# A sliding-window attention and gated MLP kernel: PSUM given out bank by bank, softmax sums of four heads together, V products in 32-column quarters, and every step's place written out

## Chip, core and metric

The kernel runs on one core of one Trainium2 chip. The metric is the device time of one execution in microseconds (us); lower is better. The kernel before takes 231.15 us, the median of three runs (230.51 to 231.65).

## What is computed

The reference, cut to what matters:

```python
# q, k, v: [8, 8, 576, 64] = batch, heads, positions, head width
scores = q @ k^T / 8                      # per batch and head
mask   = (0 <= i - j < 64)                # each position sees itself and the 63 before it
attn   = softmax(where(mask, scores, -1e9))
x      = attn @ v  -> [8, 576, 512]       # the eight heads side by side

h      = relu(x @ w_in)                   # w_in 512 x 1024
u, v2  = h[..., :512], h[..., 512:]
v_n    = (v2 - mean) / sqrt(var + 1e-6)   # per row of 512
v_s    = w_spatial @ v_n + b_spatial      # w_spatial 576 x 576, over the positions
out    = (u * v_s) @ w_out                # w_out 512 x 512, float32 [8, 576, 512]
```

Inputs and outputs are float32 in DRAM; the kernel computes in float16 with float32 sums in PSUM.

## The kernel before, in words

**Steps.** The work is cut into named steps, about 1,100 for the eight batches `b`. A step is one instruction, or for TensorE a run of matmuls. The names are used below, so here they are in the order in which a batch goes through them. A batch's eight heads come in two halves `g` of four heads; of a batch's 576 positions, 512 go in the main steps and the last 64 in steps with `r` in place of `g` ("remainder").

| step | engine | what it does | line |
|---|---|---|---|
| `ldk`, `ldq`, `ldv` | DMA on SP's queue | loads of one half's k and q (576 KB each) and v (five pieces) | L296, L320 |
| `ck`, `cq`, `cv` | POOL (also DVE, ACT in the first two batches) | float32 to float16 | L219, L217 |
| `sl`, `su`, `s4` | the same | a copy `hs` of v, shifted by 64 positions | L219 |
| `tk`, `tq` | DVE | transposes of k and q | L306 |
| `S` | PE | scores of four heads: 64 matmuls of 32x64 tiles into two PSUM tiles `sc` of two banks | L366, L430 |
| `E` | ACT | exp of a pair of heads, 128x1024, two per half | L374, L440 |
| `M` | DVE | minimum with the mask, in place, two per half | L377, L444 |
| `P` | PE | for a pair of heads: sums by a matrix of ones (`oz<-e,onesK`, two matmuls of 512 columns) and the products with v (16 matmuls of 128x64 weights, 64 columns) | L389, L394 |
| `N`, `n` | ACT | logarithm of the sums, exp of minus that: 1/sum, 128x512, one of each per pair | L409, L411 |
| `X` | DVE | product times 1/sum, gives `x` | L413 |
| `V`, `Vr`, `Vb`, `Va` | PE, ACT, DVE, DVE | second half of `x @ w_in`; relu; row statistics (two) | L506, L486, L488, L490 |
| `L1`, `L2`, `A` | ACT, ACT, DVE | 1/standard deviation, then normalised rows `vn`, five `A` | L531, L533, L543 |
| `U`, `Ur` | PE, ACT | first half of `x @ w_in`; relu | L559, L572 |
| `G`, `Ge` | PE, DVE | `w_spatial @ v_n + b`; times `u` | L589, L603 |
| `O`, `Oe`, `st` | PE, ACT, DMA | `@ w_out`; copy out of PSUM; store | L614, L477, L479 |

`V`, `U`, `G` and `O` have index 0 to 3 for full blocks of 128 and 4 for the 64-wide rest. All `A` of a batch come before its first `G`, since `G` sums over all positions. `V` and `U` need all `X` of the batch.

**Weights.** `ldwin`/`cwin` load and convert w_in (eight pieces of 256 KB), `ldwsp`/`cwsp` w_spatial, `W`/`We` transpose it on PE, `ldwo`/`cwo` load w_out. They share a staging ring `wst` of two buffers.

**Buffers.** PSUM has eight banks of 512 float32 per partition. Here four of them are two tiles `ring` of two banks each, used by turns for the scores (`sc`) and for sums and products (`oz`: bank 0 products, bank 1 sums), and four are single tiles `mm`, taken in turn by V, U, G, O and the transposes. So the four-head score step `S` takes the whole ring, and the next user waits until `E` or `X` has read it.

**What sets the order.** Each engine executes its instructions in program order and waits on semaphores. The program order is chosen by a planner (`Plan.order`, L63 to L115): a list scheduler that gives each step an estimated cost, and at each turn takes the step that could start first by these estimates and by the number of free buffers (`BUFS`, L21); ties go by a due time (`key`). Where a step may run on several engines (conversions of the first two batches) it also chooses the engine. A ring tile is given to the `S` or `P` step that the planner takes next.

Of the kernel before, what the change touches and what calls it, by code (L numbers as in the profile page):

```python
# [14 lines left out]
S = 576  # L15
BIG = 65504.0

BUFS = {"nat": 5, "natv": 3, "hqk": 3, "qkT": 6, "hv": 4, "hs": 4, "e2": 3, "ring": 2, "mm": 4,  # L21
        "lnz": 2, "zinv": 2, "x": 2, "x4": 2, "vs": 10, "st6": 6, "vn": 10, "ru": 6, "g": 10,
        "ob": 4, "wst": 2, "ln": 2}
AFTER = {"PE": 0.16, "ACT": 0.1, "DVE": 0.1, "POOL": 0.12, "DQ": 2.0}
MODE_CHANGE = 0.095


class Buf:
    __slots__ = ("tag", "users", "t", "make", "ready")

    def __init__(self, tag, make):
        self.tag, self.make, self.users, self.t = tag, make, [], None


class Op:
    __slots__ = ("engs", "key", "fn", "deps", "acq", "mode", "eng", "start", "end", "left", "outs",
                 "n", "name")

    def __init__(self, name, engs, key, fn, deps, acq, uses, mode):
        self.name, self.engs, self.key, self.fn, self.mode = name, engs, key, fn, mode  # L40
        self.acq, self.eng, self.start, self.end = acq, None, None, None
        self.deps = [d for d in deps if d is not None]
        self.outs = []
        self.left = len(self.deps)
        for d in self.deps:
            d.outs.append(self)
        for b in list(uses) + list(acq):
            b.users.append(self)


class Plan:
    def __init__(self):
        self.ops = []

    def add(self, name, engs, key, fn, deps=(), acq=(), uses=(), mode=None):
        if isinstance(engs, tuple):
            engs = [engs]
        op = Op(name, engs, key, fn, list(deps), list(acq), list(uses), mode)
        op.n = len(self.ops)
        self.ops.append(op)  # L60
        return op

    def order(self, free):  # L63
        free = dict(free)
        taken = {t: [] for t in BUFS}
        avail = [o for o in self.ops if o.left == 0]
        mode = None
        done = []
        while avail:
            best = None  # L70
            for o in avail:
                t0 = 0.0
                for d in o.deps:
                    t = d.end + AFTER[d.eng]
                    if t > t0:
                        t0 = t
                want = {}
                for b in o.acq:
                    i = len(taken[b.tag]) + want.get(b.tag, 0)
                    want[b.tag] = want.get(b.tag, 0) + 1  # L80
                    if i >= BUFS[b.tag]:
                        for u in taken[b.tag][i - BUFS[b.tag]].users:
                            if u.end is None:
                                t0 = None
                                break
                            t0 = max(t0, u.end + 0.1)
                    if t0 is None:
                        break
                if t0 is None:
                    continue  # L90
                e, c = min(o.engs, key=lambda ec: max(free[ec[0]], t0) + ec[1])
                t = max(free[e], t0)
                rank = (t, o.key, o.n)
                if best is None or rank < best[0]:
                    best = (rank, o, e, c, t)
            assert best is not None, "no step can go"

            _, o, e, c, t = best
            if e == "PE" and o.mode is not None:
                if mode is not None and o.mode != mode:  # L100
                    c += MODE_CHANGE
                mode = o.mode
            o.eng, o.start, o.end = e, t, t + c
            free[e] = t + c
            for b in o.acq:
                taken[b.tag].append(b)
            avail.remove(o)
            done.append(o)
            for x in o.outs:
                x.left -= 1  # L110
                if x.left == 0:
                    avail.append(x)
        assert len(done) == len(self.ops), "steps left over"
        done.sort(key=lambda o: (o.start, o.n if o.eng is None else 0))
        return done  # L115
# [3 lines left out]
def kernel(  # L119
# [27 lines left out]


    scratch = cpool.tile([128, 512], f16, name="scratch")
    nc.vector.memset(scratch[:], 0.0)  # L150
    warm = psp.tile([128, 512], f32, tag="mm", bufs=BUFS["mm"], name="warm")
    for _ in range(16):
        nc.tensor.matmul(warm[:, :], scratch[:, 0:128], scratch[:, :], start=True, stop=True)

    onesK = cpool.tile([128, 64], f16, name="onesK")
    nc.vector.memset(onesK[:], 1.0)
# [11 lines left out]
    maskr = cpool.tile([128, 8, 64], f16, name="maskr")  # L168
    for h in (0, 1):
        for u in range(8):  # L170
            if u % 2 == 1:
                nc.vector.tensor_copy(mask[:, h, u, :], keep[:])
            else:
                nc.vector.tensor_scalar(mask[:, h, u, :], keep[:], -1.0, BIG, ALU.mult, ALU.add)
        nc.vector.memset(mask[64:128, h, 0, :], 0.0)
    for u in range(8):
        nc.vector.tensor_copy(maskr[:, u, :], mask[:, 0, 2, :])
# [3 lines left out]
    for i in range(NSB):  # L181
        nc.vector.memset(mv_t[i][:], 1.0)
        nc.vector.memset(vn4_t[i][64:65, :], 1.0)
# [8 lines left out]
        "e2": ([128, 2, 512], f16), "lnz": ([128, 512], f32), "zinv": ([128, 512], f32),  # L192
        "x4": ([128, 256], f16), "vs": ([128, 512], f16), "st6": ([128, 8], f32),
        "vn": ([128, 512], f16), "ru": ([128, 512], f32), "g": ([128, 512], f16),
        "ob": ([128, 512], f32), "wst": ([128, 1024], f32), "ln": ([128, 10], f32),
    }

    def buf(tag, name):
        if tag == "ring":
            return Buf(tag, lambda: psp.tile([128, 2, 512], f32, tag="ring", bufs=2, name=name))  # L200
        if tag == "mm":
            return Buf(tag, lambda: psp.tile([128, 512], f32, tag="mm", bufs=BUFS["mm"], name=name))
        if tag[0] == "x" and tag != "x4":
            return Buf(tag, lambda: pool.tile([128, 512], f16, tag=tag, bufs=BUFS[tag], name=name))
        shape, d = SHAPES[tag]
        return Buf(tag, lambda: pool.tile(shape, d, tag=tag, bufs=BUFS[tag], name=name))

    for r in range(4):
        BUFS[f"x{r}x"] = 2
# [10 lines left out]


    WIN, WSP, WOUT = [], [], []

    def win_steps(key):
        for half in (1, 0):
            for r in range(4):
                st = buf("wst", f"wi{half}{r}")
                cs = slice(512 * half, 512 * half + 512)
                ld = add(f"ldwin{half}{r}", ("DQ", 0.68), key + 0.001 * (4 * (1 - half) + r),
                         lambda e, st=st, r=r, cs=cs: nc.sync.dma_start(  # L230
                             st.t[:, 0:512], moe_w_in[128 * r:128 * r + 128, cs]), acq=[st])
                WIN.append(add(f"cwin{half}{r}", [("ACT", 0.5), ("DVE", 0.43), ("POOL", 0.6)],
                               -1 + key + 0.001 * (4 * (1 - half) + r),
                               lambda e, st=st, r=r, cs=cs: cp(e, w_in_sb[r][:, cs], st.t[:, 0:512]),
                               deps=[ld], uses=[st]))

    def win_dep(half, r):
        return WIN[4 * (1 - half) + r]

    def wsp_steps(key):  # L240
        nat = []
        for t in range(5):
            tn = 128 if t < 4 else 64
            st = buf("wst", f"ws{t}")
            ld = add(f"ldwsp{t}", ("DQ", 0.75 if t < 4 else 0.4), key + 0.001 * t,
                     lambda e, st=st, t=t, tn=tn: nc.sync.dma_start(
                         st.t[0:tn, 0:576], moe_w_spatial[128 * t:128 * t + tn, :]), acq=[st])
            nat.append(add(f"cwsp{t}", [("ACT", 0.55), ("DVE", 0.47), ("POOL", 0.67)],
                           key + 0.001 * t,
                           lambda e, st=st, t=t, tn=tn: cp(e, wsp_nat[t][0:tn, :],  # L250
                                                           st.t[0:tn, 0:576]),
                           deps=[ld], uses=[st]))
        st = buf("wst", "wsb")
        ld = add("ldb", ("DQ", 0.1), key + 0.006, lambda e, st=st: nc.sync.dma_start(
            st.t[64:65, 0:576], moe_b_spatial[:].unsqueeze(0)), acq=[st])
# [389 lines left out]
    for o in order:  # L645
        for bf in o.acq:
            t = bf.make()
            if t is not None:
                bf.t = t
# [35 lines left out]
```

## Time and profile before

| what | value |
|---|---|
| runs before | 231.15, 231.65, 230.51 us |
| span of the profiled execution, first to last instruction | 228.4 us |
| median of the runs minus that span | 2.75 us |
| mean granted TensorE clock | 0.933 of full |
| busy POOL; 128x1024 exps `E` (32) on ACT | 84.1 us; 31.1 us |
| `N` of 128x512 (32) and `n` of 128x512 (32) on ACT | 19.3 and 20.4 us |
| bytes moved by DMA, mean rate | 42.67 MB, 187 GB/s |

The profile is of one execution; its own time as a run is not given apart from the span, so the 2.75 us stands for what lies around the span. "Busy" counts an instruction from start to end; matmuls overlap, so a run of matmuls is better read from one start to the next start than from the sum of durations. A "granted clock" of 0.50 in a stretch means that TensorE got half of its clock there.

Starts of `G0` of each batch in the chain that ended last and in the timeline of PE: 54.47, 78.8, 102.9, 126.3, 150.1, 173.5, 196.0 and 215.2 us. The last matmul ends near 224.7 us, and one copy and one store follow.

### The profile page before, as it was taken

How to read it: one execution, taken by the hardware profiler on the slowest of the kernel's cores; microseconds unless marked ns; L12 is line 12 of the kernel's file. 1: busy time of each engine (PE TensorE's matmuls, PEld its weight loads, DVE VectorE, ACT ScalarE, POOL GpSimd, SP SyncE). 2: the span in 40 equal slices, each digit the busy share in tenths (PEclk: the TensorE clock that was granted, in tenths of full speed). 3: DMA queues.
4: the chain of work that ended last, by engine and by line, in shares of the span. 5: the costliest groups of instructions: out<-in, count | busy, mean ns of one | idle time of the engine just before them, and what ended most of it. 6: DMA issues, size and time to landing. Idle time of an engine off the chain costs nothing.

```text
span 228.4 us, 6947 instructions
## 1 busy us (share of the span) xinstructions
PE 193.3 (85%) x2873; PEld 98.1 (43%) x2873; DVE 178.6 (78%) x341; ACT 157.1 (69%) x281; POOL 84.1 (37%) x124
## 2 busy tenths in 40 slices
PE   7413329886989997999899997999799999999993
PEld 2202224452544553454445453455345544554441
DVE  7896769998697788978989879988888686855640
ACT  3554564995469956797579676975696779758623
POOL 2001213252869645882488038913870000000000
PEclk9955556998899999999999999999999999999999
DMA  6999889799988999979689728511310041014005
GB/s 227 343 309 264 241 238 321 213 282 274 305 252 249 332 292 312 292 182 268 166 296 262 163 96 276 143 25 46 140 26 4 31 156 26 3 46 153 12 13 193
DMA packets 50417, 42.67 MB, mean 187 GB/s; under 512 B 39569, under 2 KB 39569, under 8 KB 50386
## 3 DMA queue, kind: packets, MB, share of 16 engines
q1 hardware_dynamic: 50386, 42.23, 62.8%
q8 instruction: 22, 0.36, 0.7%
q14 instruction: 9, 0.07, 0.1%
HBM read 32.79 MB, written 9.44 MB: 185 GB/s over the span
## 4 chain that ended last, share of the span: by engine, by line
PE 54%; DVE 17%; DMA 13%; ACT 8%; issue 4%; SPq 1%; POOL 0%; DVEq 0%; ACTq 0%; POOLq 0%
PE pg L589 16%; PE pv L506 8%; PE po L614 7%; PE pu L559 6%; DMA nq<-in_q_dram 6%; DVE qT L306 4%; PE sc L366 4%; DMA ws<-in_moe_w_spatial_dram 4%; DVE kT L306 3%; PE oz L389 3%; PE oz L394 2%; ACT e L374 2%; DMA wi<-in_moe_w_in_dram 2%; PE pg L595 2%; DMA wo<-in_moe_w_out_dram 2%
## 5 line engine op out<-in xcount | busy, mean ns | idle before, releaser
L219 POOL COPY hs<-hv 64x512 f16<-64x512 f16 x51 | 33.8, 665 | 25.1 <-ACT hv L217 10.6
L589 PE MATMUL pg<-wspT,vn 128*128 128x512 f16 (+1 forms) x160 | 39.4, 389 | 1.0 <-DVE vn L543 1.0
L374 ACT ACTIVATE e<-sc 128x1024 f16<-128x1024 f32 x32 | 31.1, 1022 | 4.3 <-PE sc L366 3.6
L506 PE MATMUL pv<-win,x 128*128 128x512 f16 x128 | 32.6, 395 | 0.0
L603 DVE TENSOR_TENSOR g<-pg,ru 128x512 f16<-128x512 f32 (+1 forms) x40 | 24.7, 634 | 9.1 <-PE pg L589 9.1
L377 DVE TENSOR_TENSOR e<-e,mask 128x1024 f16<-128x1024 f16 x32 | 26.8, 854 | 5.7 <-ACT e L374 5.7
L559 PE MATMUL pu<-x,win 128*128 128x512 f16 x128 | 31.0, 380 | 0.0
L477 ACT COPY ob<-po 128x512 f32<-128x512 f32 (+1 forms) x33 | 19.3, 585 | 16.4 <-PE po L614 15.4
L614 PE MATMUL po<-wout,g 128*128 128x512 f16 x128 | 30.5, 380 | 0.0
L409 ACT ACTIVATE ln<-oz 128x512 f32<-128x512 f32 x32 | 19.3, 602 | 16.1 <-PE oz L394 16.1
L488 DVE BATCH_NORM_STATS2 st<-vs 128x6 f32<-128x512 f16 (+1 forms) x40 | 26.9, 677 | 4.1 <-ACT vs L486 3.8
L486 ACT ACTIVATE vs<-pv 128x512 f16<-128x512 f32 (+1 forms) x40 | 23.5, 594 | 6.7 <-PE pv L506 5.5
L413 DVE TENSOR_TENSOR x<-oz,zi 128x512 f16<-128x512 f32 x32 | 21.8, 684 | 6.0 <-ACT zi L411 6.0
L219 POOL CAST hv<-nv 128x512 f16<-128x512 f32 x26 | 16.2, 644 | 26.7 <-DMA nv<-in_v_dram 13.8
L411 ACT ACTIVATE zi<-ln 128x512 f32<-128x512 f32 (+1 forms) x40 | 23.7, 593 | 0.9
L306 DVE STREAM_TRANSPOSE kT<-hk 128x576 f32<-128x576 f32 x16 | 20.0, 1250 | 3.6 <-PE scr L430 3.2
L366 PE MATMUL sc<-qT,kT 32*64 32x128 f16 (+2 forms) x1024 | 13.8, 231 | 9.1 <-DVE x L413 8.0
L589 PEld LDWEIGHTS <-vn 128*128 128x128 f16 (+1 forms) x160 | 13.9, 98 | 17.7 <-DVE vn L543 4.8
L572 ACT ACTIVATE ru<-pu 128x512 f32<-128x512 f32 (+1 forms) x40 | 20.6, 571 | 0.8 <-PE pu L559 0.8
L306 DVE STREAM_TRANSPOSE qT<-hq 128x576 f32<-128x576 f32 x16 | 19.9, 1244 | 0.3 <-ACT hq L217 0.3
L219 POOL CAST hk<-nk 128x1152 f16<-128x1152 f32 x12 | 13.7, 1143 | 16.7 <-DMA nk<-in_k_dram 8.5
L389 PE MATMUL oz<-e,onesK 128*64 128x512 f16 x64 | 14.1, 435 | 6.1 <-DVE e L377 6.1
(79 smaller groups left out, 274.3 us busy)
## 6 DMA issues: line engine op xcount, KB each, us to landing
nk<-in_k_dram SPq DMA_DIRECT2D x16, 576.0 KB, 5.4
nq<-in_q_dram SPq DMA_DIRECT2D x16, 576.0 KB, 6.0
nv<-in_v_dram SPq DMA_DIRECT2D x64, 128.0 KB, 5.2
out_dram<-ob SPq DMA_DIRECT2D x32, 256.0 KB, 2.2
wi<-in_moe_w_in_dram SPq DMA_DIRECT2D x8, 256.0 KB, 4.5
ws<-in_moe_w_spatial_dram SPq DMA_DIRECT2D x4, 288.0 KB, 4.2
nv<-in_v_dram SPq DMA_DIRECT2D x16, 64.0 KB, 4.2
wo<-in_moe_w_out_dram SPq DMA_DIRECT2D x4, 256.0 KB, 3.8
```

The lines of the kernel that those rows point to most:

```text
L219: ENG[e].tensor_copy(o, i)
L306: d = add(f"t{name}{b}_{g}", ("DVE", 0.68), key, lambda e: nc.vector.transpose(qt.t[:, :].rearrange("p (i j) -> p j i", j=18), h.t[:, :].b ...
L374: ex = add(f"E{b}_{g}{u}", ("ACT", 0.91), key, lambda e, u=u: nc.scalar.activation(e2[u].t[:, :, :], sc[u].t[:, :, :], AF.Exp, bias=0.0, s ...
L377: mins.append(add(f"M{b}_{g}{u}", ("DVE", 0.58), key, lambda e, u=u: nc.vector.tensor_tensor(e2[u].t[:, :, :], e2[u].t[:, :, :], mask[:, : ...
L411: c = add(f"n{b}_{r}", ("ACT", 0.09 + 0.0008 * n), key, lambda e: nc.scalar.activation(zi.t[:, 0:n], lz.t[:, 0:n], AF.Exp, bias=0.0, scale ...
L486: rl = add(f"Vr{b}_{j}", ("ACT", 0.5), key, lambda e: nc.scalar.activation(vs.t[0:jn, :], m.t[0:jn, :], AF.Relu), deps=[pv], acq=[vs], use ...
L488: s1 = add(f"Vb{b}_{j}", ("DVE", 0.7), key + 0.02, lambda e: nc.vector.bn_stats(st6.t[0:jn, 0:6], vs.t[0:jn, :]), deps=[rl], acq=[st6], us ...
L506: nc.tensor.matmul(m.t[:, :], XB[b, r].t[:, 128 * j:128 * j + 128], w_in_sb[r][:, 512:1024], start=(r == 0), stop=(r == 3))
L559: nc.tensor.matmul(m.t[:, :], w_in_sb[r][:, 128 * i:128 * i + 128], XB[b, r].t[:, :], start=(r == 0), stop=(r == 3))
L589: nc.tensor.matmul(m.t[:, :], w[0:kn, 128 * i:128 * i + 128], wspT[kk][0:kn, 0:512], start=(kk == 0), stop=(kk == 4))
L603: lambda e, m=m, g=g, ru=ru, n=n: nc.vector.tensor_tensor(g.t[:, 0:n], m.t[:, 0:n], ru.t[:, 0:n], ALU.mult),
L614: nc.tensor.matmul(m.t[:, :], G[r][0].t[:, 128 * j:128 * j + 128], w_out_sb[r][:, :], start=(r == 0), stop=(r == 3))
```

## The change

1. **PSUM** is four tiles of two banks made once (`PAIR`), and each PE step is told its banks: the number after the colon in the written order, e.g. `S0_0:PE:0:1` (two pairs: banks 0 to 3) or `P0_0:PE:6:5`. In the written order `S` always has pairs 0 and 1, and everything else shares banks 4 to 7.
2. **Sums.** A new step `Z` makes the sums of four heads in one bank: four matmuls, each with a 128x32 matrix of ones and 512 columns, into partitions 0, 32, 64 and 96 upward. `N` and `n` then run once per half, not once per pair, and both `X` of the half use the one result.
3. **V products.** `P` covers four heads: each head's v is split into even and odd columns (`vhalf`), 32 wide, so `P` is 64 matmuls of 128x32 weights and 64 columns into two banks, in place of two times 16 of 128x64. A half's `x` is one tile [128, 2, 512]; w_in's rows are loaded in the order that this gives (`(p two) c -> p two c`).
4. **Order.** `Plan.order` goes. `ORDER` is a list of all 1,029 steps, with engine and banks, that is emitted as it stands.
5. Smaller: w_in and w_out come in loads of 512 KB (six in place of twelve) and `wst` has three buffers; v of batches 2 to 7 is converted and shifted in one piece per half (4 POOL instructions in place of 7); `vs` and `vn` have 8 buffers (were 10), `e2` 4 (were 3), the remainder's `er` has 2 of its own; the mask is made in 9 instructions (were 26).

The diff, cut to its core:

```diff
+ORDER = """
+ldk0_0:DQ
+ldq0_0:DQ
+...
+S0_0:PE:0:1
+...
+"""
+def as_listed(plan):
+    by = {s.name: s for s in plan.steps}
+    out = []
+    for word in ORDER.split():
+        name, eng, *banks = word.split(":")
+        out.append((by.pop(name), eng, [int(x) for x in banks]))
+    return out
...
+    PAIR = [psp.tile([128, 2, 512], f32, name=f"ps{i}") for i in range(4)]
+    def bank(j):
+        return PAIR[j // 2][:, j % 2, :]
...
+    def vhalf(t, c, hh, f):
+        return t[:, c, hh, :].rearrange("p (d two) -> p two d", two=2)[:, f, :]
...
-        s = add(f"S{b}_{g}", ("PE", 0.5), key, emit_S, deps=[DKT[b, g], DQT[b, g], LASTP[0]],
-                acq=sc, uses=[KT[b, g], QT[b, g]], mode="s")
+        s = add(f"S{b}_{g}", ("PE", 0.53), key, emit_S, deps=[DKT[b, g], DQT[b, g]],
+                acq=sc + e2, uses=[KT[b, g], QT[b, g]], mode="s")
...
-                    for h in (0, 1):
-                        nc.tensor.matmul(oz.t[64 * h:64 * h + 64, 1, :], onesK[:, :], ee[:, h, :],
-                                         start=True, stop=True)
-                    for c in range(8):
-                        for h in (0, 1):
-                            vv = vn if c % 2 == 1 or c == 0 else vs
-                            nc.tensor.matmul(oz.t[64 * h:64 * h + 64, 0, 64 * c:64 * c + 64],
-                                             vv[:, c // 2, 2 * u + h, :],
-                                             ee[:, h, 64 * c:64 * c + 64], start=True, stop=True)
+        def emit_Z(e):
+                for hh in range(4):
+                    nc.tensor.matmul(zb.t[32 * hh:32 * hh + 32, :], ones[:, :],
+                                     e2[hh // 2].t[:, hh % 2, :], start=True, stop=True)
+        def emit_P(e):
+                for f in (0, 1):
+                    for c in range(8):
+                        vv = hv if c % 2 == 1 or c == 0 else hs
+                        for hh in range(4):
+                            nc.tensor.matmul(ob[f].t[32 * hh:32 * hh + 32, 64 * c:64 * c + 64],
+                                             vhalf(vv, c // 2, hh, f),
+                                             e2[hh // 2].t[:, hh % 2, 64 * c:64 * c + 64],
+                                             start=True, stop=True)
+        for f in (0, 1):
+            XD[b, 2 * g + f] = add(f"X{b}_{g}{f}", ("DVE", 0.61), key + 0.04,
+                lambda e, f=f: nc.vector.tensor_tensor(x.t[:, f, :], ob[f].t[:, :], lz.t[:, :],
+                                                       ALU.mult), ...)
...
-    order = plan.order({"PE": 9.0, "ACT": 2.0, "DVE": 6.0, "POOL": 4.0, "DQ": 0.0})
-    for o in order:
...
+    for s, eng, banks in CHOOSE(plan):
+        for x in s.acq:
+            if x.tag == "bank":
+                x.t = bank(banks.pop(0))
+            elif x.tag == "pair":
+                x.t = PAIR[banks.pop(0)]
+            else:
+                x.t = x.make()
+        s.fn(eng)
```

The written order of PE up to the first `G`, and of one later stretch (each with its banks left out): `S0_0 S0_1 Z0_0 P0_0 Z0_1 P0_1 S0_r V0_0 S1_0 V0_1 Z0_r V0_2 P0_r V0_3 U0_0 V0_4 S1_1 W2 Z1_0 W4 U0_1 U0_2 W1 W0 P1_0 U0_3 W3 S1_r Z1_1 P1_1 U0_4 S2_0 G0_0`; and `G3_0 G3_1 G3_2 V4_0 G3_3 V4_1 S5_1 V4_2 O3_0 O3_1 O3_2 V4_3 O3_3 Z4_r Z5_0 U3_4 G3_4 P4_r U4_0 V4_4 P5_0 S5_r U4_1 U4_2 U4_3 P5_1 Z5_1 S6_0 G4_0`. The last PE steps are `V7_4 U7_1 U7_2 U7_3 G7_0 G7_1 G7_2 G7_3 O7_0 O7_1 G7_4 O7_2 U7_4 O7_3 O7_4`.

DVE's written order ahead of G0_0 ends `tq1_1 Vb0_3 Va0_3 Vb0_4 We2 M1_10 tk2_0 Va0_1 M1_11 We4 tq2_0 Va0_4 Va0_2 Va0_0 X1_00 X1_01 We3 A0_4 A0_0 A0_1 A0_2 A0_3`. Over the bytes of the loads in their written order, `ldwsp4` (the last piece of w_spatial) ends at 9.91 MB, `ldq2_0` at 11.35 MB and `ldq3_0` at 15.49 MB.

## The prediction

> **What bounds it now.** I read the busy shares first, then the slices of the span, then stretches of 8 us, then the rows of PE and DVE in order of time.
>
> ```profile
> PE 193.3 (85%) x2873; PEld 98.1 (43%) x2873; DVE 178.6 (78%) x341; ACT 157.1 (69%) x281; POOL 84.1 (37%) x124
> PE   7413329886989997999899997999799999999993
> PEclk9955556998899999999999999999999999999999
> DMA  6999889799988999979689728511310041014005
> ```
>
> The kernel has two parts. In the first ten slices (5.7 us each) PE has little to do, on half the clock, while the loads keep the DMA engines at 80% and more. From about 54 us on PE is nearly always busy and DMA slackens towards the end. So there are two questions: how early does PE get going, and how many gaps are left after that?
>
> The start, on PE:
>
> ```profile
> 18.76 0.25 PE L394 MATMUL oz<-e,hv 128*64 128x64 f16 x2
> 22.53 0.31 PE L366 MATMUL sc<-qT,kT 32*64 32x128 f16 x2 [3.52 <-DVE x L413]
> 24.88 1.07 PE L366 MATMUL sc<-qT,kT 32*64 32x128 f16 x62 [2.04 <-DVE x L413]
> ...
> 34.63 4.32 PE L506 MATMUL pv<-win,x 128*128 128x512 f16 x12
> ...
> 54.47 2.15 PE L589 MATMUL pg<-wspT,vn 128*128 128x512 f16 x5 [0.99 <-DVE vn L543]
> ```
>
> The scores of the second half of batch 0 (S0_1) wait for X, which has to empty the PSUM ring, until 24.9 us; V0 begins at 34.6 and the first G at 54.5.
>
> The steady part, PE and then DVE around one gap:
>
> ```profile
> 69.25 0.76 PE L366 MATMUL sc<-qT,kT 32*64 32x128 f16 x64
> 69.95 0.40 PE L518 MATMUL pv<-win,x 128*64 128x512 f16 x1
> ...
> 72.76 0.41 PE L389 MATMUL oz<-e,onesK 128*64 128x512 f16 x2
> 73.00 0.23 PE L394 MATMUL oz<-e,hv 128*64 128x64 f16 x4
> ...
> 73.22 0.20 PE L394 MATMUL oz<-e,hv 128*64 128x64 f16 x2
> 73.35 1.04 PE L559 MATMUL pu<-x,win 128*128 128x512 f16 x4
> ...
> 91.55 0.30 PE L453 MATMUL ozr<-e_r,onesK 128*64 128x256 f16 x2 [1.61 <-DVE e_r L444]
> ```
>
> ```profile
> 87.36 1.26 DVE L306 STREAM_TRANSPOSE kT<-hk 128x576 f32<-128x576 f32 x1 [0.79 <-PE scr L430]
> 88.46 1.24 DVE L306 STREAM_TRANSPOSE qT<-hq 128x576 f32<-128x576 f32 x1
> 89.54 1.24 DVE L306 STREAM_TRANSPOSE kT<-hk 128x576 f32<-128x576 f32 x1
> 90.62 0.88 DVE L444 TENSOR_TENSOR e_r<-e_r,maskr 128x512 f16<-128x512 f16 x1
> ```
>
> From start to start: S takes 0.70 us (69.25 to 69.95), sums and products of a pair of heads 0.59 (72.76 to 73.35). The gap of 1.61 us is three transposes placed ahead of M_r on DVE; PE's in-order queue stands behind P_r. In the same way from starts: V 3.5 per batch, V4 0.98, U 3.46, U4 0.56, G 4.35, G4 0.61, O 3.46, two S 1.40, S_r 0.27, four P 2.36, P_r 0.36: **21.3 us of PE work per batch**. The first G of batches 0 and 6 start at 54.47 and 196.01, so a batch takes 141.5/6 = 23.6: **2.3 us of gaps per batch**.
>
> **Part 1, the products on PE.** Z is four matmuls of 512 columns into four quarters. The two of the old sums run side by side: 0.24 us for both (72.76 to 73.00). Side by side, four give 0.24; one after another in pairs 0.48. I take 0.30, with a change of tile shape. P is 64 matmuls of 64 columns with 128x32 weights, which no row shows. From below: S has 64 small matmuls in 0.70, 10.9 ns each. The old products advance by two matmuls in 0.032 (73.00 to 73.22), 16 ns each, so 64 take 1.04. From above, far off: G4's 20 matmuls of 64 columns with 128-wide weights take 0.61, 30.5 ns each, 1.95 for 64. I take 0.87, the middle of the two near rows. Z and P are then 1.17 per half, against 2 x 0.59 = 1.18 for the two old pairs: **nothing**. The bounds over 16 halves: -2.7 us (0.70), +2.7 (1.04) and +17.3 (1.95). Four times as many, narrower instructions buy PE nothing; they only bring the outputs into the partitions in which Z's sums lie. The remainder: 0.36 now, Z_r and P_r 0.1 + 16 x 13.5 ns + 0.1, the same.
>
> One rule of the Trainium skill speaks against this part: "TensorE: Matmul & The Clock Gate", section "Back-to-back issue gap", gives a floor of about 25 ns from start to start however few the columns. S's rows, with 10.9 ns, are below it, at least on separate tiles. By the rule P would be 1.6 us, 16 x 0.73 = 11.7 us more than I take, and the time 227.
>
> **Part 2, sums of four heads at once.** 16 of the 32 N (602 ns) and 16 of the 32 n (637 ns) go, 19.8 us of ACT, and half of each remainder pair. ACT is 69% busy, so I count nothing for its own sake: where it is fullest (7.7 of 8 us around 72 to 80) PE is full as well. X, M, Ge, Vb and the transposes on DVE stay as many as before; 78% with overlaps leaves DVE second.
>
> **Part 3, the start.** S has banks 0 to 3 to itself, so S0_1 no longer waits for X. In the new order it needs only tq0_1: that transpose starts at 11.17 now, and POOL's casts (1.15 each) in place of ACT's move it to about 11.5. So S0_1 is near 12.5 in place of 24.9, the X are done near 23 and V0 starts near 24. Then the loads decide. The bytes moved, summed from the rates of stretches of 4 us, are 6.8 MB at 24 us, 9.85 at 36 and 11.1 at 40. w_spatial is complete at 9.91 MB, 36 us, and ldq2_0 at 11.35 MB, about 41.4. From there on DVE, in its written order: cast of q on POOL 1.15, tq2_0 1.09, three Va 0.35, two X 1.2, We3 0.4, five A 1.65: **G0_0 at 47.3**. PE by itself would get there at 45.3 (w_spatial at 36.5, then 8.3 us of W, U, P, Z, S and a start). -7.2 us. SP's queue has one added wait on the way: ldwin01 needs the staging buffer that cwin100 on ACT empties, placed after n0_0, near 19.5 us; k1_1 and w_spatial queue behind it. 0.5 MB is still under way then, so I count nothing; if that cover is gone, all loads move by the delay, 1 to 2 us.
>
> Before that G the new order has done more of batches 1 and 2: two old P (1.18), S1_r (0.27) and S2_0 (0.70): **-2.15**.
>
> **Part 4, the steady part.** I walked the written order from G3_0 to G4_0 with start-to-start times of before (matmul blocks 0.87, G 1.08, E 0.91, M and X 0.6, transposes 1.09). Only four banks, 4 to 7, now serve all but S, so each block waits for whoever emptied the bank last, and in that walk they are empty in time: Ge3_0 comes after a transpose and two X on DVE, 2.9 us after G3_0's start, and its bank 7 is next wanted by G3_3 at 4.1. M_r is not behind three transposes any more, and S and Z stand ahead of the steps that wait. The walk from G2_0 to G3_0 gives 0.5 us of waiting (P4_0 for Ge2_4, at the end of DVE's row). The walk leaves out the slowing of M next to POOL copies (854 ns on average, 693 the median) and the delays between engines that don't fit the sum. I take **0.8 us of gaps per batch** in place of 2.3, from a walk with 0 to 0.5 and some price for what it leaves out: 6 x 1.5 = **-9.0**. The ends: 0.3 (-3 more) and the present 2.3 (+9).
>
> **Part 5, the end.** Now the V of batch 7 end at 211.3 and the last A at 215.6; four U and U4 cover that. In the new order V7_4 stands before only three U (2.6 us), so G7_0 waits 4.3 - 2.6 = 1.7; and G7_4 no longer stands between G7_3 and O7_0, so Ge7_3's 0.9 us opens: **+2.6**. The last copy and store (224.8 to 228.4) stay.
>
> **At no price:** fewer mask instructions (DVE was done with them at 5.7 us, the first cast of k ended at 6.1), larger w_in loads, fewer and longer POOL copies (POOL 37%), smaller `vs` and `vn`. Stores queue among loads on SP; the loads run more than a batch ahead (S3_1's q at 17.9 MB is wanted near 68 us, moved by 64). If that cover is thin, a batch needs 4.7 MB in 22 us, 214 GB/s, and the slices show up to 340.
>
> **The sum.** 228.4 - 7.2 - 2.15 - 9.0 + 2.6 = 212.65 for the span, and with 2.75 around it (231.15 median less the span) **215.4 us**.
>
> **Rivals.**
> - *The gaps stay, or the head start does.* Bank waits on four banks take the place of the ring's, or the A chain of batch 0 still ends at 54. For: DVE is 78% busy and in written order, and any M held up by POOL shifts everything behind. Against: the walk. Without Part 4's gain 224.4; without Part 3's first term 222.6. Chance 0.21.
> - *Slower: narrow products cost as much as G4's.* At 30.5 ns a matmul PE gets 17.3 us more: **232.7**. It takes place in P, on the engine that sets the period. It decides from 0.87 + 15.75/16 = 1.85 us per P on, 29 ns a matmul. For: the only rows with 64 columns that reload weights for one use with 128 rows are at 16 to 35 ns. Against: S's 10.9 ns. Chance 0.10, with other ways to be slower.
> - *All bounds good:* P at 0.70, gaps 0.3, G0_0 at 45.3: 215.4 - 2.7 - 3 - 2 = 207.7. Chance 0.11.
>
> That the change doesn't do what it says would show as shared banks serialised by tile and not by bank; the waits that PE gets in the built program are few, so I give that no case of its own.
>
> My forecast has 0.58. The range takes in the good case and the first rival and leaves out the slower one: 206 to 227. Within 0.5% (1.2 us) of 231.15, about what a measurement can tell, I put 0.04, slower 0.10, faster 0.86.
>
> **What would show it.** Right: S0_1 before 15 us and V0 before 27; G0_0 at 45 to 49; 22 us from G to G; Z and P together 1.0 to 1.35; idle PE ahead of G7_0 and O7_0 of some 1.7 and 0.9. Wrong: P over 1.4 us; PE idle behind DVE (X, Ge) or ACT on banks 4 to 7 by more than 1.5 us a batch; G0_0 after 51, behind the loads or the A.

## The result, and the profile after

The changed kernel takes **248.49 us** (median of five runs, 248.03 to 251.28) against 231.15 (five runs, 229.47 to 231.80): 1.080 times the time before, 95% interval 1.073 to 1.086. The forecast was 215.4, with a range up to 227. The profiled execution has a span of 249.6 us. Runs of one kernel differ by up to 3%, and the profiles of e1, e4, e8 and e9 are of slow runs, so below the medians (all runs) and the ratios to the kernel before (fast runs alone) compare times, and profiles serve for where the waits are.

The page after, in its busy shares and slices (6.24 us each):

```profile
PE 195.0 (78%) x3465; PEld 97.7 (39%) x3465; DVE 169.1 (68%) x299; ACT 134.9 (54%) x251; POOL 91.1 (36%) x111
PE   7324758549887988887978798789888898899882
PEclk9956797956999999997999999999999999999998
DMA  7998989897069928977932008910658122003114
```

No engine has much more to do: PE went from 193.3 to 195.0 us, DVE and ACT fell. Most of PE's 9s of before have become 7s and 8s, all the way to the end, so the time is in many gaps. Adding up the waits of 0.15 us or more ahead of PE's rows gives 49.5 us after and 31.3 before. The G0 of the eight batches start at 56.56, 82.99, 106.23, 136.50, 163.82, 188.24, 213.45 and 233.43. Of the 21.2 us between the spans, 2.1 lie ahead of the first G, 16.3 between the first and the last (25.27 us a batch in place of 22.94), 2.8 behind.

The start, on PE:

```profile
11.84 0.77 PE L1364 MATMUL ps<-qT,kT 32*64 32x128 f16 x64 [2.33 <-DVE qT L1300]
...
48.61 0.52 PE L1261 MATMUL ps<-id,wnat 128*128 128x128 f16 x5 [1.74 <-ACT ru L1592]
...
52.25 0.75 PE L1364 MATMUL ps<-qT,kT 32*64 32x128 f16 x30
55.98 0.65 PE L1364 MATMUL ps<-qT,kT 32*64 32x128 f16 x34 [2.99 <-issue]
56.56 4.69 PE L1609 MATMUL ps<-wspT,vn 128*128 128x512 f16 x12
```

S0_1 at 11.84 is where the forecast had it. W3 (48.61) waits for a `Ur`, and S2_0 stops after 30 of its 64 matmuls for 3 us, with nothing named that it waits for.

The steady part, around the first O, on PE and then on ACT:

```profile
64.48 1.04 PE L1523 MATMUL ps<-win,x 128*128 128x512 f16 x4
65.81 1.02 PE L1523 MATMUL ps<-win,x 128*128 128x512 f16 x4 [0.29 <-DVE g L1623]
66.67 1.02 PE L1635 MATMUL ps<-wout,g 128*128 128x512 f16 x4
68.87 1.89 PE L1635 MATMUL ps<-wout,g 128*128 128x512 f16 x8 [1.17 <-ACT vs L1503]
```

```profile
64.60 1.94 ACT L1371 ACTIVATE e<-ps 128x1024 f16<-128x1024 f32 x2
67.74 1.09 ACT L1503 ACTIVATE vs<-ps 128x512 f16<-128x512 f32 x2 [1.20 <-PE ps L1635]
```

The rows in order are V1_1 (bank 7), V1_2 (bank 4), O0_0 (bank 6), O0_1 and O0_2 (banks 5 and 7). On ACT, Vr1_1 reads bank 7. V1_1 was complete by 65.5 and ACT free from 66.54, but Vr1_1 starts at 67.74, when O0_0 has been written, and the releaser named is L1635, O's line: bank **6**. Then O0_1 wants bank 5, whose last reader is Ge0_3 on DVE, done by 66.4. It starts at 68.87, when the second `Vr` of the row, Vr1_2, has read bank **4** (67.74 + 1.09 = 68.83). Neither waits for its own bank; each waits for the other bank of the same two-bank tile.

Sums and products of one half, from Z to the next step:

```profile
127.58 0.40 PE L1383 MATMUL ps<-e,ones 128*32 128x512 f16 x4
127.81 0.29 PE L1469 MATMUL ps<-er,hs 128*32 128x64 f16 x16
129.15 0.24 PE L1399 MATMUL ps<-e,hv 128*32 128x64 f16 x8 [1.05 <-DVE g L1623]
...
129.61 0.22 PE L1399 MATMUL ps<-e,hv 128*32 128x64 f16 x4
129.76 0.40 PE L1537 MATMUL ps<-win,x 128*64 128x512 f16 x1
```

Z takes 0.23 us (127.58 to 127.81), the 64 products of P 0.61 (129.15 to 129.76): 9.5 ns a product. The time is not lost here.

### The profile page after: what moved, and what is told of

Same layout as the page of the kernel before. It is cut to its first block, busy times and chain, and to the rows that moved or that the text cites. A ratio compares the mean times of both kernels' runs of the same rounds, so it can differ in the third digit from the quotient of the medians.

```text
span 249.6 us, 7996 instructions
## 1 busy us (share of the span) xinstructions
PE 195.0 (78%) x3465; PEld 97.7 (39%) x3465; DVE 169.1 (68%) x299; ACT 134.9 (54%) x251; POOL 91.1 (36%) x111
## 5 line engine op out<-in xcount | busy, mean ns | idle before, releaser
L1609 PE MATMUL ps<-wspT,vn 128*128 128x512 f16 (+1 forms) x160 | 39.3, 394 | 4.7 <-DVE x L1408 1.4
L1503 ACT ACTIVATE vs<-ps 128x512 f16<-128x512 f32 (+1 forms) x40 | 23.6, 598 | 34.4 <-PE ps L1523 19.4
L1371 ACT ACTIVATE e<-ps 128x1024 f16<-128x1024 f32 x32 | 31.7, 1023 | 16.7 <-PE ps L1364 16.5
L1623 DVE TENSOR_TENSOR g<-ps,ru 128x512 f16<-128x512 f32 (+1 forms) x40 | 24.6, 629 | 22.7 <-PE ps L1609 14.1
L1523 PE MATMUL ps<-win,x 128*128 128x512 f16 x128 | 33.5, 388 | 4.7 <-DVE x L1408 3.0
L1579 PE MATMUL ps<-x,win 128*128 128x512 f16 x128 | 31.1, 379 | 6.3 <-ACT ru L1592 2.4
L1635 PE MATMUL ps<-wout,g 128*128 128x512 f16 x128 | 33.4, 395 | 3.2 <-ACT vs L1503 1.6
L1505 DVE BATCH_NORM_STATS2 st<-vs 128x6 f32<-128x512 f16 (+1 forms) x40 | 26.6, 678 | 13.7 <-ACT vs L1503 13.7
L1494 ACT COPY ob<-ps 128x512 f32<-128x512 f32 (+1 forms) x40 | 22.9, 585 | 22.5 <-PE ps L1635 12.8
L1592 ACT ACTIVATE ru<-ps 128x512 f32<-128x512 f32 (+1 forms) x40 | 21.6, 553 | 15.0 <-PE ps L1635 5.4
L1196 POOL COPY hs<-hv 64x768 f16<-64x768 f16 (+3 forms) x33 | 28.4, 860 | 2.8 <-PE ps L1469 1.3
L1196 POOL CAST hk<-nk 128x1152 f16<-128x1152 f32 x15 | 17.2, 1148 | 27.6 <-DVE st L1505 12.5
L1609 PEld LDWEIGHTS <-vn 128*128 128x128 f16 (+1 forms) x160 | 15.5, 100 | 25.6 <-issue 6.8
L1196 POOL CAST hv<-nv 128x1024 f16<-128x1024 f32 (+1 forms) x16 | 15.8, 987 | 22.4 <-DMA nv<-in_v_dram 10.1
L1399 PE MATMUL ps<-e,hv 128*32 128x64 f16 x640 | 12.5, 204 | 9.4 <-ACT lz L1414 5.8
```

What stands on the lines that cost most here:

```text
L1196: ENG[e].tensor_copy(o, i)
L1371: ex = add(f"E{b}_{g}{u}", ("ACT", 0.91), key, lambda e, u=u: nc.scalar.activation(e2[u].t[:, :, :], sc[u].t[:, :, :], AF.Exp, bias=0.0, s ...
L1494: cpy = add(f"Oe{b}_{j}", ("ACT", 0.49), key, lambda e: nc.scalar.copy(ob.t[rows, :], m.t[rows, :]), deps=[po], uses=[m, ob])
L1503: rl = add(f"Vr{b}_{j}", ("ACT", 0.49), key, lambda e: nc.scalar.activation(vs.t[0:jn, :], m.t[0:jn, :], AF.Relu), deps=[pv], uses=[m, vs])
L1505: s1 = add(f"Vb{b}_{j}", ("DVE", 0.6), key + 0.02, lambda e: nc.vector.bn_stats(st6.t[0:jn, 0:6], vs.t[0:jn, :]), deps=[rl], acq=[st6], us ...
L1523: nc.tensor.matmul(m.t[:, :], xr(b, r)[:, 128 * j:128 * j + 128], w_in_sb[r][:, 512:1024], start=(r == 0), stop=(r == 3))
```

## The experiments

G0_0 is the start of the first G, in us of the profile.

| kernel | median us | ratio to before (95%) | G0_0 | per batch, G0_0 to G7_0 |
|---|---|---|---|---|
| before | 231.15 | | 54.47 | 22.94 |
| after | 248.49 | 1.073 to 1.086 | 56.56 | 25.27 |
| e1 after, four single banks | 229.49 (225.91 to 232.21) | 0.974 to 0.996 | 54.62 | 23.03 |
| e2 before, `mm` as two pairs | 241.33 | 1.037 to 1.050 | | |
| e2c before, `mm` as four static tiles | 231.87 | 1.000 to 1.009 | | |
| e3 e1, stores issued by ACT | 231.38 | 0.992 to 1.002 | 52.85 | 22.72 |
| e4 e1, P in 32 products (incomplete) | 220.67 | 0.951 to 0.964 | 56.48 | 21.58 |
| e5 e1's parts, order by the planner | 221.37 | 0.941 to 0.963 | 48.66 | 22.41 |
| e6 e1, two steps of the start moved | 227.01 | 0.976 to 0.989 | 49.48 | 23.06 |
| e7 e1, 48 more opening matmuls | 223.83 (one run) | | 52.93 | 22.08 |
| e8 e5 with two-bank tiles | 254.69 | (250.4 to 255.0 us) | 54.47 | 26.09 |
| e9 e5, P in 32 products (incomplete) | 222.66 | 0.945 to 0.961 | 51.55 | 22.42 |

### e1: single banks

The theory after the result: a wait goes by PSUM tile, not by bank. The rivals stand with each expectation.

```diff
-    PAIR = [psp.tile([128, 2, 512], f32, name=f"ps{i}") for i in range(4)]
+    PAIR = [psp.tile([128, 2, 512], f32, name=f"ps{i}") for i in range(2)]
+    ONE = [psp.tile([128, 512], f32, name=f"bk{j}") for j in range(4, 8)]
     def bank(j):
-        return PAIR[j // 2][:, j % 2, :]
+        return ONE[j - 4][:, :]
```

> Banks 4 to 7 become four PSUM tiles of one bank each, in place of two tiles of two banks; written order, banks and all instructions stay as in the changed kernel (248.5 us, span 249.6). Theory A (waits go by the tile and not by the bank, so a step on bank 4 also waits for the reader of bank 5, and so on): the gaps of PE between G0 of batches 0 and 6 fall from about 5 us to 1 or 2 us per batch, and the time falls by 20 us or more, to 215 to 228 us. Theory B (four banks for all steps but S are too few, or the written order doesn't fit the real durations): the same waits stay with other names, 243 to 250 us.

Same steps, same order, same banks: 229.49, **19.0 us less** than the changed kernel by the medians, 22 by the two ratios to the kernel before (0.985 and 1.080). The same stretch on PE, then on ACT:

```profile
62.63 1.90 PE L1524 MATMUL bk<-win,x 128*128 128x512 f16 x8
64.37 2.75 PE L1636 MATMUL bk<-wout,g 128*128 128x512 f16 x12
66.96 1.03 PE L1524 MATMUL bk<-win,x 128*128 128x512 f16 x4
```

```profile
64.58 1.09 ACT L1504 ACTIVATE vs<-bk 128x512 f16<-128x512 f32 x2
```

V1_1 and V1_2, three O and V1_3 run through without a wait, and Vr1_1 and Vr1_2 run from 64.58 on, while O0_0 is being written. From V1_1 to V1_3 it is 4.33 us (62.63 to 66.96) against 6.11 (64.48 to 70.59).

But 229 is not 215, and it is a little above the 215 to 228 that was expected: the first six periods take 23.80 us each, with 3.2 of gaps where 1 to 2 were expected. Four of PE's waits are stops inside steps, with nothing named that releases them, 9.4 us in all:

```profile
54.04 0.65 PE L1365 MATMUL ps<-qT,kT 32*64 32x128 f16 x34 [2.82 <-issue]
108.36 2.33 PE L1636 MATMUL bk<-wout,g 128*128 128x512 f16 x10 [1.76 <-issue]
123.01 0.23 PE L1435 MATMUL ps<-qT,kT 32*64 32x64 f16 x6 [2.67 <-issue]
151.83 0.39 PE L1384 MATMUL bk<-e,ones 128*32 128x512 f16 x2 [2.12 <-issue]
```

### e2 and e2c: the same pairing put into the kernel before

```diff
+    MMP = [psp.tile([128, 2, 512], f32, name=f"mmp{i}") for i in range(2)]
+    MMN = [0]
+    def mm_next():
+        j = MMN[0] % 4
+        MMN[0] += 1
+        return MMP[j // 2][:, j % 2, :]
...
-            return Buf(tag, lambda: psp.tile([128, 512], f32, tag="mm", bufs=BUFS["mm"], name=name))
+            return Buf(tag, mm_next)
```

e2c is the control: four static tiles `[128, 512]`, `return MMP[j][:, :]`.

> The kernel before with its four mm banks as two static tiles of two banks, taken in the same rotation, planner and everything else untouched. Theory A: two blocks that follow each other now share a tile, so each V, U, G, O waits for the evacuation of its neighbour, and the time rises by 8 us or more, 240 to 265 us. Theory B: waits go by the bank, the time stays within 1% of 231.

> Control to the paired one: the kernel before with its four mm banks as four static tiles of one bank, the same rotation. Both theories: 231 us within 1%. If it differs, static tiles by themselves change something.

The kernel before loses 10 us when its four `mm` banks become two tiles of two banks, and under 1% when they become four static ones. So it is the pairing, not the giving out by hand.

### e3: the stores off SP's queue

```diff
-        lambda e: nc.sync.dma_start(out[b, dst, :], ob.t[rows, :])
+        lambda e: nc.scalar.dma_start(out[b, dst, :], ob.t[rows, :])
```

> As with single bank tiles, and the stores are issued from ACT's queue and no longer from SP's, so no load stands behind a store that waits for its copy. If the stores among the loads on SP's queue cost time (SP waits 110 us for the output copies in the changed kernel), it is 3 us or more faster than single bank tiles alone. If not, it is the same, or slower by ACT's time for issuing 40 stores (0.3 to 0.6 us each on SP now).

231.38 (ten runs) against 229.49: no gain. SP's stores wait long for `ob` (110 us after, 65 before), but taking them off the queue of the loads does not shorten the time.

### e4: half as many products

```diff
-                    for c in range(8):
-                        vv = hv if c % 2 == 1 or c == 0 else hs
+                    for c in range(0, 8, 2):
+                        vv = hv if f == 0 or c == 0 else hs
...
-                                             e2[hh // 2].t[:, hh % 2, 64 * c:64 * c + 64],
+                                             e2[hh // 2].t[:, hh % 2, 64 * c:64 * c + 128],
```

> The kernel of e1_single_banks (four single banks, written order), with P as 32 products of 128 columns in place of 64 of 64 columns: as many columns stream, half as many instructions. It leaves out the alternation of the two copies of v from one 64-column piece to the next. Theory 'instruction count': the stops of 2 to 3 us in the middle of a step, with nothing shown that they wait for (9.4 us in the profile of e1_single_banks), come from the number of PE instructions, which P has raised. Then they fall below 5 us, and the time falls by 4 to 8 us from the 229.5 of e1_single_banks, to 221 to 226. Rival 'not P': the stops have another cause; P itself is 0.6 us a pair at 8 ns a product, and half of its instructions can save at most 0.3 us a pair, under 5 us over 16 pairs; the stops stay between 7 and 12 us and the time within 227 to 231.

e4 reads one copy of v for each pair of 64-column pieces where the full computation alternates between two, so it is a test of the number of instructions and not a kernel to use.

220.67. Of the four stops only the first is left (2.67 us, at 56.08). The time is 8.8 us less than e1's by the medians and 6.4 by the ratios; the stops that went are 6.7. The shorter P gives little of it. One P and the start of the step behind it, in e1 and then in e4:

```profile
82.65 0.24 PE L1400 MATMUL bk<-e,hv 128*32 128x64 f16 x8
...
83.27 0.64 PE L1585 MATMUL bk<-x,win 128*128 128x64 f16 x16
```

```profile
121.86 0.46 PE L1400 MATMUL bk<-e,hv 128*32 128x128 f16 x20
122.16 0.34 PE L1400 MATMUL bk<-e,hs 128*32 128x128 f16 x12
122.43 0.61 PE L1610 MATMUL bk<-wspT,vn 128*128 128x512 f16 x2
```

64 products take 0.62 us here and 32 take 0.57, with a change of tile shape behind them; without one it is 0.50 (98.08 to 98.58 in e1) and 0.46 (97.82 to 98.28 in e4). That is about 0.05 a half, 1 us over 16 halves.

The counts of matmuls ahead of the stops say what the stops are. The rows give busy times and counts from 0 to the named time in e1; the first (x...) is PE's matmuls:

```profile
0.00:53.90 53.90, 30.87 (x735) 16.82 (x735) 37.24 (x70) 29.05 (x52) 26.60 (x41) 0.76 0.94 281
0.00:108.30 108.30, 80.99 (x1631) 41.04 (x1631) 84.93 (x147) 61.99 (x111) 58.64 (x75) 0.86 0.86 254
0.00:122.90 122.90, 92.95 (x1887) 47.67 (x1887) 95.59 (x166) 72.76 (x130) 66.74 (x84) 0.88 0.86 254
0.00:151.70 151.70, 119.66 (x2399) 60.84 (x2399) 118.00 (x205) 91.02 (x166) 74.58 (x92) 0.89 0.78 230
```

735, 1631, 1887 and 2399 are all 95 more than a multiple of 128. The two stops of the changed kernel come at 735 and 2399, e3's at 735, e4's at 607.

### e7: the boundary moved

```diff
-    for i in range(16):
-        nc.tensor.matmul(bank(4 + i % 2), scratch[:, 0:128], scratch[:, :], start=True, stop=True)
+    for i in range(64):
+        nc.tensor.matmul(ONE[i % 2][:, 0:128], scratch[:, 0:128], scratch[:, 0:128], start=True,
+                         stop=True)
```

> The kernel of e1_single_banks with 64 opening matmuls of 128 columns instead of 16 of 512: the same columns, 48 more matmuls ahead of everything else. In the kernels so far every stop for nothing shown comes after 95 + 128 k matmuls (735, 1631, 1887 and 2399 of e1_single_banks; 735 and 2399 of the changed kernel; 607 of e4_half_products). Theory 'instructions arrive 128 matmuls at a time': the stops stay at counts of 95 + 128 k and so come 48 matmuls earlier in the work: the one in the middle of S2_0 moves into P1_1. Rival 'the stop belongs to the step': it stays in the middle of S2_0, at a count of 783.

```profile
0.00:25.50 25.50, 11.88 (x351) 10.32 (x351) 14.88 (x30) 11.28 (x17) 12.39 (x23) 0.76 0.93 278
0.00:50.70 50.70, 29.07 (x735) 19.24 (x735) 39.45 (x69) 28.91 (x51) 26.98 (x41) 0.83 0.96 290
0.00:75.00 75.00, 51.28 (x1119) 30.73 (x1119) 60.28 (x103) 44.06 (x79) 41.29 (x57) 0.86 0.89 269
0.00:120.50 120.50, 95.12 (x2015) 53.24 (x2015) 101.73 (x169) 76.40 (x139) 68.24 (x84) 0.92 0.87 260
```

On PE, the stop at count 735:

```profile
47.11 0.20 PE L1401 MATMUL bk<-e,hv 128*32 128x64 f16 x2
50.83 0.21 PE L1401 MATMUL bk<-e,hv 128*32 128x64 f16 x2 [3.52 <-issue]
```

The stops stay at 95 + 128 k and move in the work: S2_0 is free of one, and P1_1 now stops two matmuls before its end. There are again four, 10.0 us in all, three of them at other boundaries than in e1. A stop belongs to the place in PE's instruction stream, not to the step. The one run of e7, 223.83, is below the fastest of e1's four (225.91) with as many stops: PE's other waits add up to 17.6 us against 25.6 in e1's profile. So a stop does not always come off the end one for one, and how much of e4's gain is due to the stops is not shown to the microsecond.

### e5, e8, e9: the planner in place of the written order

e5 has e1's tiles and all other parts of the change, but the steps are ordered by the planner of the kernel before, with banks 4 to 7 in rotation. e8 gives e5 the two-bank tiles back, with the lines of e1 reversed. e9 is e5 with e4's edit, in e5's order.

```diff
-CHOOSE = as_listed
+CHOOSE = planned
...
+            if b.tag == "bank":
+                banks.append(4 + k % 4)
```

> The kernel of e1_single_banks with all its new parts (sums of four heads, products in quarters, single banks), but its steps ordered by the planner of the kernel before, banks 4 to 7 given out in rotation, in place of the written order. Theory 'the order is what is left': once the banks are freed one by one, the written order keeps the six middle periods at 23.4 to 23.8 us because its durations are not those of the chip; the planner does no worse: 222 to 229 us. Rival 'the order carries its part': the written bank choice is what keeps the gaps where they are, and rotation makes each product wait for the oldest bank: 233 us or more.

> The kernel of e5_planner with banks 4 to 7 as two tiles of two banks again, as in the changed kernel; the planner still counts four separate banks. Theory 'waits go by tile': the two tiles make each product wait for the reader of the neighbouring bank; with rotation neighbours are used one right after the other, so the loss is at least the 9.5 us that the kernel before lost: 230 us or more against the 221.4 of e5_planner. Rival 'only the written order is hurt by it', because its choice of banks leaves neighbours to slow readers: within 3 us of 221.4.

> The kernel of e5_planner, in the same order, with P as 32 products of 128 columns as in e4_half_products (it leaves out the alternation of the two copies of v between neighbouring 64-column pieces). In e5_planner no stop of 0.3 us or more for nothing shown is left, so only the shorter P can gain: 0.43 us in e4_half_products against 0.61, 0.18 over 16 halves, 2.9 us at most. Theory 'half the instructions helped e4_half_products by its stops': e9_planner_half gains 0 to 3 us against the 221.4 of e5_planner, 218 to 221. Rival 'short products cost more than their own time': it gains as much as e4_half_products did, about 9 us, to 212 or 213.

e5 takes 221.37, the best complete version: 0.952 of the kernel before (0.941 to 0.963). With the same parts and single banks, the planner's order is thus 8 us faster than the written one (e1, 0.974 to 0.996): writing every step's place out brought nothing here. Its waits on PE of 0.15 us or more add up to 23.3 us, and none of 0.3 us or more is a stop without a releaser, though it has the same 3,465 matmuls. With two-bank tiles (e8) it takes 254.69: **33 us** for the pairing, by the medians and by the fastest runs (250.44 and 217.43) alike. e9 cannot be told from e5: where there are no stops to take away, half as many products gain nothing that shows.

### e6: the start

```diff
-cv1_11:ACT
+cv1_11:POOL
...
-S2_0:PE:1:0
 A0_2:DVE
...
 G0_0:PE:5
+S2_0:PE:1:0
```

> The kernel of e1_single_banks with two places of the written order changed at the start: cv1_11 goes from ACT to POOL, and S2_0 stands behind G0_0 instead of ahead of it. Theory 'the load holds ACT': in e1_single_banks cv1_11 waits 2.7 us on ACT for its load, Ur0_2 stands behind it, W3 waits 2.1 us for the bank that Ur0_2 reads, and We3 and the five A follow. Then W3 starts near 45.5 instead of 47.6, the last A ends near 49 instead of 51.3, and G0_0 starts near 51 instead of 54.6; the time falls by 2 to 4 us against the 229.5 of e1_single_banks. Rival 'the start was not on the path': G0_0 moves, but batch 2, whose scores come later, gives it back by its first G, and the time stays within 1 us.

```profile
45.83 0.52 PE L1262 MATMUL bk<-id,wnat 128*128 128x128 f16 x5
...
49.48 0.59 PE L1610 MATMUL bk<-wspT,vn 128*128 128x512 f16 x2
50.59 1.41 PE L1610 MATMUL bk<-wspT,vn 128*128 128x512 f16 x3 [0.51 <-DVE vn L1564]
```

W3 starts at 45.83, as expected, so its wait was the named one. G0_0 starts at 49.48 and then waits inside for one of the five A, which take 3.58 us. The time went from 229.49 to 227.01, but the two intervals overlap (0.976 to 0.989 and 0.974 to 0.996): that a start 5 us earlier is worth 2 to 4 us is not shown. PE does not stop at count 735 any more, which it now passes at 52.27.

## Why the prediction was wrong

**The failed step is in Part 4:** "each block waits for whoever emptied the bank last, and in that walk they are empty in time". The walk gave every bank its own reader. In the kernel, banks 4 and 5, and 6 and 7, are one tile each, and reader and writer of a tile wait for the readers and writers of both halves. With the rows of this profile a batch has 20.6 us of PE work (21.3 less twice the 0.34 of Part 1 below), so 26.15, the mean of the first six periods, has 5.5 us of gaps where I put 0.8. Taking the pairing out gives 19 to 22 us back under the written order and 33 under the planner; putting it into the kernel before costs 10. The last remark of the rivals named just this and dismissed it, because PE's waits are few in the built program. That counts waits where their length matters: a wait on a shared tile is one wait too, only longer. Chance and range had no place for it: "slower" had 0.10, for narrow products, and the kernel is slower for another reason. The Trainium skill asks for less than the kernel does: by "PSUM — Partial Sum Buffer", section "PSUM bank collisions raise a hardware error", PSUM is to be guarded by bank and quadrant, by bank in the simple version. e1, guarded by bank, is 19 us faster than the same order guarded by pair.

It is not the whole miss. The span is 37 us longer than the 212.65 of the sum: 9.3 ahead of the first G, 26.6 in the next six periods, 1 behind them. e1 takes 14.1 of those 26.6 away; 6.5 of the 12.5 that stay are stops, for which the sum had no term either, and the rest is waits that the walk left out.

**Part 1** put the gain too low: P 0.61 us where I took 0.87 (0.50 to 0.66 in the halves without a wait), Z 0.23 where I took 0.30; together 0.34 less than the two old pairs, 16 x 0.34 = 5.4 us less for PE, better than my best bound (2.7). The rival "narrow products cost as much as G4's" (30.5 ns) fell: 9.5 ns. So did the rule weighed there ("TensorE: Matmul & The Clock Gate", section "Back-to-back issue gap"), for products that go in turn to four column quarters. What I did not price is that 592 more matmuls (3,465 against 2,873) are more of PE's instructions to bring in: the stops, 4.7 us in the changed kernel's profile, 9.4 in e1's, none before.

**Part 2**: ACT's busy time fell by 22.2 us. That this is worth nothing by itself, as I had it, was not tried.

**Part 3** was right in its first half: S0_1 at 11.84 (12.5), V0 at 26.10 (24). G0_0 came at 56.56 instead of 47.3. Two terms failed. I took a load as there once the bytes ahead of it in SP's order had been moved, and followed the chain on DVE alone. On ACT the cast of v's piece waits longer:

```profile
47.45 0.62 ACT L1194 CAST hv<-nv 128x512 f16<-128x512 f32 x1 [2.22 <-DMA nv<-in_v_dram]
47.97 0.59 ACT L1592 ACTIVATE ru<-ps 128x512 f32<-128x512 f32 x1
```

The load ends at 11.88 MB of the order, moved by 43.7 us by this profile's rates, but lands near 47.4, 7.8 us after it was issued: the bytes of several loads are under way together. Ur0_2 stands behind that cast, W3 waits for Ur0_2's bank, then We3 and the five A. The second term is the stop in S2_0. With both taken away G0_0 is at 49.48 (e6). The wait on SP's queue that I counted as nothing lasted longer than 1 to 2 us:

```profile
SPq L1220 <- ACT win L1194: 4.6, 1, 4.6
```

It was nearly covered, though: 10.9 MB had been moved at 40 us where I had 11.1. And "-7.2" was put into the sum in full. Whether an early first G comes off the end one for one stays open: e4 gets to 220.67 with G0_0 at 56.48 and e5 to 221.37 with 48.66, but in other orders or with other stops, and e6 against e1 is too close to tell.

**Part 5** came out in its size, in part by luck: 2.8 us more behind G7_0's start, 2.6 forecast. The two waits that I named are 1.75 us: G7_0 1.12 (1.7), the O of batch 7 0.63 (0.9). The last O waits a further 0.95 for the copy ahead of it, which no term had. And the last thing that G7_0 waits for is not an A but Ur7_3 on ACT, which reads bank 7:

```profile
233.43 4.62 PE L1609 MATMUL ps<-wspT,vn 128*128 128x512 f16 x20 [1.12 <-ACT ru L1592]
```

In e1 the same wait is 0.69 us, and for an A.

**The sum.** Over the first six periods, as in the forecast (batch 6 of the kernel before has its first G at 195.94, not 196.01, which changes nothing), a batch takes 26.15 us after, 23.80 without the pairing (e1) and 22.11 with most of the stops gone too (e4). The last is the forecast's 22.1 (21.3 of work and 0.8 of gaps), but by luck: it is 20.5 of work, with the shorter P, and 1.6 of gaps. So the walk put the gaps at half of what they are even in a kernel whose banks wait one by one. e4 at 220.67 and e5 at 221.37 lie in the range; 215.4 was reached by none. The rival "the gaps stay" (224.4) is nearest to e1, not to the changed kernel.

## What to carry over

Before a walk through buffers, look at what the waits are tied to: two banks in one tile are one buffer, whatever numbers the order gives them, and a slow reader of one half holds the other half. Test a suspicion that costs a few lines to state with a price (here: what is late next if banks wait in pairs), instead of dismissing it by the number of waits. Fewer, larger instructions can have a worth that busy time does not show: where PE gets through its instructions sooner than the next ones are brought in, it stops.

## What the runs showed of the hardware

- **Instructions come in lots of 128 matmuls.** All 15 such stops of 1.2 to 3.6 us, and one of 0.65, in the changed kernel, e1, e3, e4, e6 and e7 come at a count of 95 + 128 k. The instruction queue's packets go with it: 27 for 3,465 matmuls (27.07 x 128), 23 for 2,953 (23.07 x 128), 22 for 2,873 (22.4 x 128). The rows (packets, MB, share) after, of e4 and before:

```profile
q8 instruction: 27, 0.44, 0.8%
```

```profile
q8 instruction: 23, 0.38, 0.7%
```

```profile
q8 instruction: 22, 0.36, 0.7%
```

  The traces also hold when each packet was moved, and that shows that late packets make the stops. In e1 the packets that belong to the four stops end at 52.57, 107.08, 121.61 and 150.48 us, and PE goes on at 54.04, 108.36, 123.01 and 151.83. At all 16 stops PE goes on 1.27 to 1.61 us after its packet's end. At none of the 289 boundaries of the twelve profiles does PE go on earlier than 0.9 us after it. e5 passes its boundaries without a stop because PE comes to each of them late enough, the closest 1.39 us after the packet; e6 passes count 735 at 1.74 us after it. Why some packets come late stays open.
- **Products on four column quarters** of 32 go at 7.8 ns for 64 columns (64 in 0.50 us, e1) and 14.3 ns for 128 (32 in 0.46, e4), start to start, where the next step has the same tile shape; with a change of shape behind them it is 9.5 to 9.7 ns (0.61 to 0.62) and 17.8 (0.57).
- The same `A` instruction (128x512) takes 0.39 to 1.31 us in the changed kernel, 0.40 to 0.72 before. POOL copies often run beside the long ones; this was not tried by itself.
